# Seven-product MLP2 extended from the last two groups to groups 2 to 5, with accumulator banks seeded by ScalarE copies

## The chip, the cores and the metric

One core of one Trainium2 chip. The metric is the device time of one execution in microseconds (us). With one core there is no second die to compare, so a run is called slow here only when it lies over 1.5% above the fastest of its kernel. The kernel before takes 373.25 us (median of the 3 runs before the prediction, 373.15 to 373.69). Times in the profile count from the first instruction of the span, which is about 2 us shorter than the run.

Names: PE is the TensorE matmul engine, DVE is VectorE, ACT is ScalarE, POOL is GpSimd, SP is SyncE, which issues most DMAs. PSUM is the memory in which PE accumulates; it is handed out in tiles, here of two banks each. The granted clock is the share of full speed at which PE's clock ran. Groups are counted from 0 to 7 as in the code; the words of the change count them from 1, so its "groups 3 to 6" are 2 to 5 here.

## The reference

```python
x = A_x                                          # 1 x 2048 x 576, bf16
h = x + A(layernorm(x), wqkv, wo)                # dilated local attention: 32 heads, window 8, step 2
y = layernorm(layernorm(h))                      # the MLP normalises its input once more
h2 = h + gelu(y @ w1 + b1) @ w2 + b2             # w1: 576 x 4608, w2: 4608 x 576
```

The 2048 rows are 16 tiles of 128. A group is two of these tiles. For each of the 8 groups PE does MLP1 (324 matmuls, in four visits; ACT applies the Gelu), then Wo, the attention's output projection, for the next group (36), then MLP2. LN2 is the doubled layernorm: its rows go through the DMA that transposes them (`hnT`) into the next MLP1. Attention for the group after that runs on DVE at the same time.

## The kernel before: the parts that matter

MLP2 of a group multiplies hidden blocks by the w2 blocks of one "block row", 18 times over:

    | A11 A12 |   | B11 B12 |      A: 2 tiles x 2 hidden blocks,  B: 2 hidden blocks x 2 halves of the columns
    | A21 A22 | x | B21 B22 |

Plainly that is 8 matmuls a block row, 144 a group. The Strassen-Winograd scheme needs 7 products, so 126 a group. It pays with sums of hidden blocks and weight blocks on DVE, and with partial results that two output quarters share. The kernel before has this scheme in groups 6 and 7 only. Where a quarter is to continue from a partial sum, ACT copies the PSUM bank into another bank, in which PE goes on accumulating ("seeding").

```python
    # mlp2_fast of the kernel before, groups 6 and 7 (cut)
        call(ahead[:1])                                   # Wo of the next group
        af, b = (psum_pair(tag, "po") for tag in tags[:2])
        if not last:
            product(1, af[:, 0, 0:HALF], True)
            nc.scalar.copy(out=b[:, 0, 0:HALF], in_=af[:, 0, 0:HALF])     # seed b from bank a
        call(ahead[1:])                                   # LN2 of the next group
        ...
        ce, d = (psum_pair(tag, "po") for tag in tags[2:])    # b and d are two tiles
        bank = {1: a, 2: a, 3: f, 4: c, 5: d, 6: b, 7: e}
        then = {1: [c_(nc.scalar.copy, b, a)], 6: [c_(nc.scalar.copy, d, b)], ...}
        if last:
            order = [(1, 0, cut), (4, 0, cut), (1, cut, NM), (4, cut, NM)] + [(n, 0, NM) for n in (7, 6, 2, 5, 3)]
        else:
            order = [(n, 0, NM) for n in (4, 2, 6, 7, 5, 3)]   # product 4, in bank c, stands between 1 and 2
```

```python
    # the loop over the groups, groups 2 to 5 (cut)
                    ...
                    m1[1] = [c_(att_qk_pair, e, f)]
                    ia[0] = [c_(exps, e, f), wo, c_(ln2_pair, c, d, (e, f)), ...]
            mlp1(g, "pair", m1, mid)
            mlp2_tile(g, 0, "D", ia)          # 72 plain matmuls each
            mlp2_tile(g, 1, "C", ib)
    def exps(*js):
        att_exp(*js)          # ACT: Exp, with its table load
        gelu_table()          # ACT: a tiny Gelu, which loads the Gelu table again
```

## Time and profile before

| | before |
|---|---|
| time, median | 373.25 us |
| span of the profiled run, granted clock | 370.7 us, 1.00 |
| PE busy; matmuls | 98%; 4944 |
| a plain group: MLP1, Wo, MLP2 | 17.79, 2.21, 17.75 us |
| MLP2 of group 6 (126 matmuls) | 15.54 us |
| DVE busy in the MLP2 of groups 2 to 5 | 14.7 to 16.4 of 17.7 to 18.2 us |

The page of the kernel before, its busy times and two rows of its 40 slices (a digit is tenths of a slice; PEclk is the granted clock):

```profile
PE 363.6 (98%) x4944; PEld 299.1 (81%) x4944; DVE 286.9 (77%) x415; ACT 225.5 (61%) x499; POOL 41.1 (11%) x47
PE   8999999999999999999999999999999999999996
PEclk9999999999999999999999999999999999999999
```

All that PE waited for, in the list of waits (total, times, longest):

```profile
PE busy L695 <- DVE prod L688: 1.5, 1, 1.5
PE pm L214 <- ACT hT L524: 0.5, 1, 0.5
PE o_pt L181 <- DVE h L432: 0.5, 1, 0.5
PE pm L214 <- DMA hnT<-td: 0.5, 1, 0.5
PE pq L214 <- ACT kv_ring L299: 0.2, 1, 0.2
```

PE is the limit: 3.2 us of waits in 370.7. A matmul taken out there is time won, as long as PE isn't made to wait. What ACT does around the end of MLP1: its timeline in group 3, where PE's MLP1 ends and Wo starts at 202.44 (start, duration, what):

```profile
200.74 4.49 ACT L524 ACTIVATE hT<-pm,b_sb 128x256 bf16<-128x256 f32 x12 [1.99 <-PE pm L214]
205.25 1.28 ACT L366 ACT_TABLE_LOAD   x1
206.54 0.63 ACT L366 ACTIVATE logits<-logits 128x512 f32<-128x512 f32 x1
207.19 1.28 ACT L497 ACT_TABLE_LOAD   x1
208.49 0.20 ACT L497 ACTIVATE warm<-mhalf 128x1 f32<-128x1 f32 x1
```

ACT ends its Gelus 2.8 us after PE ends MLP1, and is then taken by the exponentials until 6.25 us after it. In this kernel nobody waits for that: PE goes on with Wo and the plain MLP2. And where the kernel before does seed a bank (group 6), PE doesn't wait either. The copy, in ACT's timeline, and PE's matmuls under it:

```profile
320.80 0.39 ACT L621 COPY po<-po 128x288 f32<-128x288 f32 x1 [1.82 <-PE po L610]
```

```profile
320.05 0.65 PE L610 MATMUL po<-w2b_sb,hT 128*128 128x288 bf16 x4
320.54 1.14 PE L610 MATMUL po<-kv_ring,hT 128*128 128x288 f16 x8
```

The matmuls from 320.54 on are product 4, which has a bank of its own.

### The profile page before, as it was taken

How to read it: one execution, taken by the hardware profiler on the slowest of the kernel's cores; microseconds unless marked ns; L12 is line 12 of the kernel's file. 1: busy time of each engine (PE TensorE's matmuls, PEld its weight loads, DVE VectorE, ACT ScalarE, POOL GpSimd, SP SyncE). 2: the span in 40 equal slices, each digit the busy share in tenths (PEclk: the TensorE clock that was granted, in tenths of full speed). 3: DMA queues.
4: the chain of work that ended last, by engine and by line, in shares of the span. 5: the costliest groups of instructions: out<-in, count | busy, mean ns of one | idle time of the engine just before them, and what ended most of it. 6: DMA issues, size and time to landing. Idle time of an engine off the chain costs nothing.

```text
span 370.7 us, 11474 instructions
## 1 busy us (share of the span) xinstructions
PE 363.6 (98%) x4944; PEld 299.1 (81%) x4944; DVE 286.9 (77%) x415; ACT 225.5 (61%) x499; POOL 41.1 (11%) x47
## 2 busy tenths in 40 slices
PE   8999999999999999999999999999999999999996
PEld 4689877888788877887788778877887888778884
DVE  6799999999999959999686989598959883532332
ACT  2688755798738790679166915692468436735630
POOL 2322004000220011003100011001100210000000
PEclk9999999999999999999999999999999999999999
DMA  7969798956557725600471145313820361030001
GB/s 230 316 180 307 190 200 229 336 181 75 173 168 137 257 87 85 102 18 34 104 120 51 34 104 105 66 33 99 106 53 18 85 121 37 0 88 19 4 0 32
DMA packets 60722, 42.51 MB, mean 115 GB/s; under 512 B 31728, under 2 KB 58992, under 8 KB 60672
## 3 DMA queue, kind: packets, MB, share of 16 engines
q1 hardware_dynamic: 58784, 39.95, 40.8%
q0 software_dynamic: 1728, 1.77, 4.8%
q8 instruction: 38, 0.62, 0.7%
q10 hardware_dynamic: 160, 0.07, 0.1%
q14 instruction: 12, 0.10, 0.1%
HBM read 19.92 MB, written 12.42 MB: 87 GB/s over the span
## 4 chain that ended last, share of the span: by engine, by line
PE 80%; DVE 14%; ACT 2%; DMA 1%; issue 1%; SPq 1%; POOL 0%; DVEq 0%; POOLq 0%
PE pm L214 35%; PE po L539 24%; PE po L610 8%; PE pq L214 6%; PE pw L214 4%; DVE prod L332 2%; DVE prod L381 2%; DVE prod L326 2%; DVE prod L385 2%; PE busy L695 1%; ACT hT L524 1%; DVE x_all L573 1%; DMA hnT<-td 1%; PE xt_pt L181 1%; DVE peak L344 1%
## 5 line engine op out<-in xcount | busy, mean ns | idle before, releaser
L524 ACT ACTIVATE hT<-pm,b_sb 128x256 bf16<-128x256 f32 (+1 forms) x288 | 108.6, 497 | 86.8 <-PE pm L214 86.8
L214 PE MATMUL pm<-hnT,w_sb 64*128 64x256 bf16 x2304 | 143.0, 269 | 0.9 <-ACT hT L524 0.5
L214 PEld LDWEIGHTS <-w_sb 64*128 64x128 bf16 x2304 | 112.4, 94 | 15.6 <-issue 2.1
L539 PEld LDWEIGHTS <-hT 128*128 128x128 bf16 x864 | 84.0, 98 | 22.6 <-issue 1.7
L539 PE MATMUL po<-w2a_sb,hT 128*128 128x288 bf16 x672 | 84.5, 286 | 0.0
L214 PE MATMUL pq<-wq_sb,xnT 64*128 64x288 bf16 x768 | 54.3, 283 | 0.3 <-ACT kv_ring L299 0.2
L214 PEld LDWEIGHTS <-xnT 64*128 64x128 bf16 x864 | 43.9, 94 | 9.3 <-ACT xnT L260 0.4
L326 DVE TENSOR_TENSOR prod<-kv_ring,q_all 128x4608 bf16<-128x4608 bf16 x16 | 40.8, 2549 | 13.2 <-DMA kv_ring<-kv_dram 13.1
L381 DVE TENSOR_TENSOR prod<-kv_ring,probs 128x4608 bf16<-128x4608 bf16 x16 | 40.9, 2558 | 7.8 <-DMA kv_ring<-kv_dram 7.4
L332 DVE TENSOR_TENSOR prod<-prod 128x2304 bf16<-128x2304 bf16 (+1 forms) x64 | 44.2, 691 | 2.1
L214 PE MATMUL pm<-hnT,w1h_sb 64*128 64x256 bf16 x288 | 39.3, 269 | 0.0
L448 POOL TENSOR_TENSOR ln_rstd<-ln_var,mhalf 128x1 f32<-128x1 f32 x14 | 16.1, 1151 | 190.3 <-ACT ln_var L447 190.3
L385 DVE TENSOR_TENSOR prod<-prod 128x2304 bf16<-128x2304 bf16 (+1 forms) x32 | 33.9, 1058 | 1.1
L539 PE MATMUL po<-w2b_sb,hT 128*128 128x288 bf16 x192 | 25.5, 286 | 0.0
L299 ACT CAST kv_ring<-pq 128x576 bf16<-128x576 f32 x32 | 19.5, 642 | 8.2 <-PE pq L214 8.2
L586 DVE TENSOR_TENSOR prod<-hT 128x512 f16<-128x512 f16 (+1 forms) x8 | 3.7, 458 | 21.6 <-ACT hT L524 21.6
L214 PE MATMUL pw<-wo_sb,oT 64*128 64x288 bf16 x256 | 19.5, 283 | 0.2
L161 POOL TENSOR_TENSOR ln_rstd<-ln_veps,mhalf 128x1 f32<-128x1 f32 (+2 forms) x13 | 13.3, 1026 | 49.3 <-DVE ln_veps L155 40.3
L214 PEld LDWEIGHTS <-oT 64*128 64x128 bf16 x288 | 13.9, 94 | 4.3 <-POOLq L224 0.8
L469 POOL DMA_DIRECT2D x_all<-h x12 | 10.9, 1060 | 44.4 <-DMA td<-q_all 30.2
L214 PEld LDWEIGHTS <-w1h_sb 64*128 64x128 bf16 x288 | 14.1, 94 | 1.6
L150 DVE BATCH_NORM_STATS2 ln_stats<-x_all 128x6 f32<-128x288 bf16 x32 | 12.8, 443 | 2.4 <-DMA x_all<-in_A_x_dram 2.4
(99 smaller groups left out, 326.3 us busy)
## 6 DMA issues: line engine op xcount, KB each, us to landing
w_sb<-in_B_w_dram SPq DMA_DIRECT2D x6, 768.0 KB, 6.1
kv_ring<-kv_dram SPq DMA_DIRECT2D x28, 144.0 KB, 2.6
w2a_sb<-in_B_w_dram SPq DMA_DIRECT2D x4, 1008.0 KB, 6.5
kv_dram<-kv_ring SPq DMA_DIRECT2D x13, 288.0 KB, 4.6
out_dram<-o_sb SPq DMA_DIRECT2D x15, 144.0 KB, 3.1
td<-q_all SPq DMA_DIRECT2D x14, 144.0 KB, 2.0
td<-hn SPq DMA_DIRECT2D x14, 144.0 KB, 1.8
wq_sb<-in_A_wqkv_dram SPq DMA_DIRECT2D x3, 576.0 KB, 6.6
```

The source lines that it names most:

```text
L150: nc.vector.bn_stats(out=stats[:, i, c, :], in_=src[:, c * HALF:(c + 1) * HALF])
L161: nc.gpsimd.tensor_tensor(out=rstd[:], in0=veps[:], in1=mhalf[:].to_broadcast([P, n]), op=ALU.pow)
L214: last = nc.tensor.matmul(duo["g"][r ^ swap][i], lhsT=lhsT, rhs=rhs, start=(swap == 0 and i == 0 and kt == 0), stop=(swap == 1 and kt == K ...
L299: pace[0] = nc.scalar.copy(out=dst.rearrange("p (d g h) -> p g d h", g=2, h=H // 2), in_=ps[:, :, 0:HALF].rearrange("p g (h d) -> p g d h" ...
L326: nc.vector.tensor_tensor(out=prod[:], in0=k_ring[j % 2], in1=q_all[:, j, :].unsqueeze(1) .to_broadcast([P, W, D]), op=ALU.mult)
L332: nc.vector.tensor_tensor(out=prod[:, :, o * H:o * H + n], in0=prod[:, :, a * H:a * H + n], in1=prod[:, :, c * H:c * H + n], op=ALU.add)
L381: nc.vector.tensor_tensor(out=prod[:].rearrange("p w (d h) -> p w d h", h=H), in0=v_ring[j % 2].rearrange("p w (d h) -> p w d h", h=H), in ...
L385: nc.vector.tensor_tensor(out=prod[:, 0:n, :], in0=prod[:, 0:n, :], in1=prod[:, n:2 * n, :], op=ALU.add)
L448: nc.gpsimd.tensor_tensor(out=rstd[:], in0=var[:], in1=mhalf[:], op=ALU.pow)
L524: pace[0] = nc.scalar.activation(out=hT[us[i // GF]][:, GF * r + i % GF, 0:N], in_=ps[:, r, i * N:(i + 1) * N], func=ACT.Gelu_apprx_tanh, ...
L539: nc.tensor.matmul(banks[half], lhsT=hT[f // (2 * GF)][:, f % (2 * GF), i * P:(i + 1) * P], rhs=w2_rows(f)[:, half * HALF:(half + 1) * HAL ...
L610: nc.tensor.matmul(bank, lhsT=l, rhs=r, start=(start and m == 0), stop=(m == NM - 1), skip_group_check=True)
```

## The change

The intent: seven products for the first 8, 8, 12 and 12 of the 18 block rows of groups 2 to 5 too, 40 matmuls fewer. The rest of the diff finds room for it: weight sums partly in place of a w2 quarter or in odd slots of x (so x of the odd tiles is loaded again later, into even slots), hidden sums partly in place, one sum taken in each group. All seven-product groups now use five banks in three PSUM tiles, with three seeds each, instead of six banks in four tiles.

```diff
+    def x_of(j):
+        return x_all[:, j - j % 2, :]
+    def reload_x(js):
+        for j in js:
+            nc.sync.dma_start(out=x_of(j), in_=x3[:, j, :])
...
-    fast = GROUPS[-2:]
+    fast = GROUPS[2:]
...
+        af, bd, ee = (psum_pair(tag, "po") for tag in tags)
+        a, f, b, d = (pair[:, n, 0:HALF] for pair in (af, bd) for n in range(2))
+        e = ee[:, 0, 0:HALF]
...
+        product(1, a, rows, True)
+        seed(b, a)                      # nc.scalar.copy
+        call(inserts.get(1, ()))        # LN2 statistics, hidden sums
+        product(2, a, rows)             # the same bank a
+        plain(0, 0, a, rows)            # the block rows that stay plain
...
+        product(6, b, rows)
+        seed(d, b)
+        call(inserts.get(6, ()))        # LN2 rows normalised (ACT) and sent
+        product(7, e, rows, True)
...
+        product(5, d, rows)
+        seed(f, d)
+        product(4, b, rows)
+        plain(1, 0, b, rows)
+        plain(1, 1, d, rows)
...
+        product(3, f, rows)
+        plain(0, 1, f, rows)
...
+        ROWS = {2: 8, 3: 8, 4: 12, 5: 12, 6: NM, 7: NM}
...
+            mlp1(g, mlp1_plan(p, q, r, s, True), m1, mid)
+            if e is not None:
+                exps(e, f)
+            if c is not None:
+                wo_visit((c, q), (d, r))
+            mlp2_fast(g, rows, (s, p, q), c is None, x)
```

## The prediction

> **What bounds it now.** TensorE: the busy summary gives PE 98% of a 370.7 us span, granted clock 9 or more in all slices, and the list of waits finds only 3.2 us of PE waiting. A plain group of two block rows is 37.7 us by the chain (MLP1 17.79, Wo 2.21, MLP2 17.75: 144 matmuls, so 123 ns each). The two seven-product groups need 126 matmuls, 15.54. VectorE is busy 31 to 33 of 37.7 us in each of the groups 2 to 5 (counted from 0; table of windows), ScalarE 23.
>
> **Removed.** With r of 18 rows by seven products a group has 144 - r matmuls: r = 8, 8, 12, 12 saves 40, at 123 ns 4.9 us (estimate from the above). All of it lies on the critical path. The 0.5 us PE wait for the transposed LN2 rows before group 6 should also go.
>
> **Added, off the path.** Sums of hidden blocks on VectorE: 0.42 us for 512 elements and 0.55 for 768, so about 0.69 and 0.95 at 1024 and 1536; four per group, 2.8 to 3.8 us. The weight sums only move; those in group 1 (6 x 0.75) fill its 4.2 us wait for the exponentials. VectorE ends near 300 us in all. Reloads of x: four groups, 2 x 144 KB each, at a DMA share of about 0.35. Seed copies: 18 of 0.385 us.
>
> **Added, on the path.** The first seed is the flaw. Product 1 is followed directly by product 2 into the same bank, but ScalarE has to copy that bank in between, so PE waits for it. The present kernel runs product 4 meanwhile. And in groups 2 to 5 ScalarE comes late: its timeline in group 3 shows the last Gelu ending 2.8 us after MLP1's last matmul (202.44 to 205.25), then two table loads around the exponentials (1.28 + 0.63 + 1.28 + 0.20) until 208.7. The Trainium skill's page "ScalarE: Activation LUTs", section "What ACT_TABLE_LOAD costs", gives about 1283 ns for one; this trace agrees (1283 ns). The copy stands behind all that: free at +6.3, done at +6.65, PE on at about +6.75. PE reaches it at 2.2 (Wo) + 1.0 (8 matmuls) = +3.2, or +3.7 with 12. Stall 3.55, 3.55, 3.05, 3.05: 13.2 us. Group 6 has no exponentials: product 1 ends at +4.4, copy and handshake about 0.65. Group 7: no Wo either, product 1 complete only near the last Gelu, +1.1.
>
> Sum: 373.25 - 4.9 - 0.5 + 13.2 + 1.75 = 382.8.
>
> **Prediction:** 382.8 us, 8 in 10 between 378 and 387. Faster by over 2%: 0.03; within 2%: 0.20; slower by over 2%: 0.77.
>
> **What would show it.** In the list of waits, PE waits for the ScalarE seed copy, six times: four of 3 to 3.6 us, two near 1. The chain passes in groups 2 to 5 from PE through the last Gelus, both table loads, the exponentials and the copy back to PE. PE has 40 fewer matmuls at an unchanged 123 ns spacing. VectorE idles longer than before in these groups. The next group's MLP1 doesn't wait for VectorE's output sums.
>
> **What would make it wrong.** ScalarE being less late than I reckon would bring it near 376. VectorE's order (output sum behind the weighted sums of V, 5.2 us) is within about 1 us of holding the second MLP1 visit; if it does, add 1 to 2 us a group. The skill's "TensorE: Matmul & The Clock Gate", Part 1, has the clock drop after an idle window of about 3.4 us; the stalls are that long, and the clock row would show it. If the copy doesn't hold product 2 at all, about 369.

## The result, and the profile after

The change is slower: 392.85 us median (389.87 to 396.85, 4 runs, one of them slow) against 373.2 for the kernel before (4 runs). The ratio is 1.0504 (95% interval 1.0424 to 1.0584). A ratio is the mean time of one kernel's fast runs over that of the other's of the same rounds, so not quite the ratio of the medians. The direction was predicted; the size was not: 19.6 us lost for 9.6 predicted. The granted clock of the four runs, 0.995, 0.977, 0.990 and 0.977, goes roughly with their times, 389.87, 394.31, 391.39 and 396.85.

The profiled run is the fastest of them. Its busy times and slices:

```profile
PE 361.8 (93%) x4904; PEld 297.3 (77%) x4904; DVE 298.3 (77%) x412; ACT 229.8 (59%) x513; POOL 35.1 (9%) x47
PE   7999999999999998968998799979997999999895
PEclk9999999999999999989999999999999999999999
```

There are 40 matmuls fewer, and PE is busy 93% instead of 98%. PE's waits:

```profile
PE po L619 <- ACT po L650: 17.2, 12, 3.3
PE busy L721 <- DVE prod L714: 1.5, 1, 1.5
PE po L619 <- ACT h_all L528: 1.4, 1, 1.4
PE pm L214 <- DVE o_sb L692: 1.0, 1, 1.0
...
```

Line 650 is the seed copy. PE waits for it twelve times, not six. PE's own timeline shows where, in groups 2 and 3 (the idle time before a piece stands in brackets):

```profile
167.44 1.16 PE L619 MATMUL po<-w2a_sb,h_all 128*128 128x288 bf16 x8
171.89 4.28 PE L619 MATMUL po<-w2a_sb,h_all 128*128 128x288 bf16 x20 [3.29 <-ACT po L650]
...
181.10 0.65 PE L619 MATMUL po<-x_all,h_all 128*128 128x288 f16 x4 [1.00 <-ACT po L650]
...
214.95 2.61 PE L619 MATMUL po<-w2a_sb,h_all 128*128 128x288 bf16 x20 [3.30 <-ACT po L650]
```

The piece at 167.44 is product 1, that at 171.89 product 2. So the first wait is there as predicted. The piece at 181.10 is product 4, whose wait the prediction does not have. And the same 20 matmuls take 4.28 us in group 2 and 2.61 in group 3: in group 2 the clock has fallen. The table of windows shows it (window, its length, then busy us and instructions of PE, PEld, DVE, ACT and POOL, granted clock, DMA share, GB/s):

```profile
168.97:172.39 3.42, 0.50 (x5) 0.39 (x5) 3.38 (x6) 3.38 (x7) 0.00 (x0) 1.00 0.24 86
172.39:175.80 3.41, 3.41 (x17) 2.18 (x15) 2.59 (x4) 3.15 (x10) 0.56 (x1) 0.50 0.00 0
```

PE was idle for 2.92 us of the first window, and in the second it ran at half the clock. ACT's timeline for the first wait has the chain that the prediction named, in the place of the five lines shown of before (PE's MLP1 ended at 165.2):

```profile
163.60 4.49 ACT L528 ACTIVATE h_all<-pm,b_sb 128x256 f16<-128x256 f32 x12 [1.99 <-PE pm L214]
168.11 1.28 ACT L366 ACT_TABLE_LOAD   x1
169.40 0.63 ACT L366 ACTIVATE logits<-logits 128x512 f32<-128x512 f32 x1
170.05 1.28 ACT L504 ACT_TABLE_LOAD   x1
171.34 0.20 ACT L504 ACTIVATE warm<-mhalf 128x1 f32<-128x1 f32 x1
171.45 0.39 ACT L650 COPY po<-po 128x288 f32<-128x288 f32 x1
```

And for the wait of product 4, the third copy behind the two LN2 rows:

```profile
178.17 0.38 ACT L650 COPY po<-po 128x288 f32<-128x288 f32 x1 [2.50 <-PE po L619]
178.47 0.30 ACT L460 ACTIVATE ln_nmean<-ln_nmean,ln_rstd 128x1 f32<-128x1 f32 x1
178.80 0.87 ACT L174 ACTIVATE hn<-h,ln_nmean,ln_rstd 128x576 bf16<-128x576 f32 x1
179.57 0.28 ACT L460 ACTIVATE ln_nmean<-ln_nmean,ln_rstd 128x1 f32<-128x1 f32 x1
179.88 0.87 ACT L174 ACTIVATE hn<-h,ln_nmean,ln_rstd 128x576 bf16<-128x576 f32 x1
180.66 0.39 ACT L650 COPY po<-po 128x288 f32<-128x288 f32 x1
```

Product 4 writes bank b; that copy only reads bank d and writes bank f. In the built program, product 5 waits until ACT's counter has reached 221 (the second copy, which fills d), and product 4 until it has reached 226: the four LN2 instructions and the third copy. Banks b and d are the two halves of one PSUM tile, `bd`.

The stages that changed, each from its first matmul to the first of the next stage (us, worked out from the matmuls' start times in the traces; the experiments' columns are used below):

| stage | before | after | control | fill | fill + split | product 1 twice |
|---|---|---|---|---|---|---|
| MLP2, group 2 | 17.75 | 23.06 | 22.73 | 21.56 | 20.39 | 18.62 |
| MLP2, group 3 | 17.75 | 21.39 | 23.05 | 21.56 | 20.39 | 18.62 |
| MLP2, group 4 | 17.75 | 19.88 | 19.87 | 20.04 | 19.41 | 17.75 |
| MLP2, group 5 | 18.27 | 19.88 | 21.54 | 20.04 | 19.41 | 17.75 |
| MLP2, group 6 | 15.54 | 16.86 | 16.86 | 16.86 | 16.22 | 16.22 |
| group 7 to the end | 36.84 | 39.59 | 39.57 | 39.58 | 38.95 | 38.96 |

The 18.27 of before holds its wait of 0.5 us for the LN2 rows of group 6.

The ideal for groups 2 and 3 is 136 matmuls at 0.123 us, 16.8 us, and 16.3 for 4 and 5 (estimates from the spacing before).

### The profile page after: what moved, and what is told of

It reads as the page before. It is cut to its first block, busy times and chain, and to the rows that moved or that the text cites. A ratio compares the mean times of both kernels' runs of the same rounds, so it can differ in the third digit from the quotient of the medians.

```text
span 388.1 us, 11433 instructions
## 1 busy us (share of the span) xinstructions
PE 361.8 (93%) x4904; PEld 297.3 (77%) x4904; DVE 298.3 (77%) x412; ACT 229.8 (59%) x513; POOL 35.1 (9%) x47
## 4 chain that ended last, share of the span: by engine, by line
PE 51%; DVE 32%; ACT 7%; issue 4%; DMA 2%; SPq 1%; POOL 1%; DVEq 0%; ACTq 0%; POOLq 0%
PE pm L214 25%; PE po L619 24%; DVE prod L381 5%; DVE prod L332 5%; DVE prod L326 5%; DVE prod L385 4%; ACT h_all L528 3%; DVE ln_stats L150 2%; PE pw L214 2%; DVE h L439 1%; DMA x_all<-in_A_x_dram 1%; ACT po L650 1%; ACT L504 1%; DVE peak L344 1%; PE pq L214 1%
## 5 line engine op out<-in xcount | busy, mean ns | idle before, releaser
L528 ACT ACTIVATE h_all<-pm,b_sb 128x256 f16<-128x256 f32 (+1 forms) x288 | 108.5, 498 | 94.4 <-PE pm L214 94.4
L619 PEld LDWEIGHTS <-h_all 128*128 128x128 f16 x560 | 55.1, 99 | 36.3 <-issue 22.2
L619 PE MATMUL po<-w2a_sb,h_all 128*128 128x288 bf16 (+1 forms) x332 | 47.3, 293 | 14.7 <-ACT po L650 13.3
L542 PEld LDWEIGHTS <-h_all 128*128 128x128 bf16 x288 | 28.0, 98 | 7.7 <-issue 0.7
L542 PE MATMUL po<-w2a_sb,h_all 128*128 128x288 bf16 x224 | 28.3, 286 | 0.0
L455 POOL TENSOR_TENSOR ln_rstd<-ln_var,mhalf 128x1 f32<-128x1 f32 x14 | 10.3, 733 | 198.2 <-ACT ln_var L454 196.8
L619 PEld LDWEIGHTS <-kv_ring 128*128 128x128 f16 x228 | 22.3, 98 | 5.6
L599 DVE TENSOR_TENSOR kv_ring<-h_all 128x1536 f16<-128x1536 f16 (+2 forms) x8 | 6.3, 786 | 21.4 <-ACT h_all L528 21.4
L619 PE MATMUL po<-w2b_sb,h_all 128*128 128x288 bf16 (+1 forms) x152 | 22.2, 286 | 0.0
L650 ACT COPY po<-po 128x288 f32<-128x288 f32 x18 | 6.9, 386 | 19.8 <-PE po L619 19.8
```

The source lines that it names most:

```text
L455: nc.gpsimd.tensor_tensor(out=rstd[:], in0=var[:], in1=mhalf[:], op=ALU.pow)
L528: pace[0] = nc.scalar.activation(out=hT(grp)[:, f, 0:N], in_=ps[:, r, i * N:(i + 1) * N], func=ACT.Gelu_apprx_tanh, bias=b1_sb[:, f:f + 1] ...
L542: nc.tensor.matmul(banks[half], lhsT=hT(grp)[:, f, i * P:(i + 1) * P], rhs=w2_rows(f)[:, half * HALF:(half + 1) * HALF], start=(f == 0), s ...
L619: nc.tensor.matmul(bank, lhsT=l, rhs=r, start=start, stop=stop, skip_group_check=True)
L650: nc.scalar.copy(out=to, in_=bank)
```

## The experiments

The theory after the traces: the loss has three parts, (A) the wait for the first copy, as predicted; (B) a wait of product 4 that comes of two banks sharing one tile; (C) a TensorE clock that falls because of the waits. Rivals: the scatter and the extra loss come from the work that the change added elsewhere (DVE sums, x reloads, DMA queue), or product 4 really needs that copy. All ten kernels gave correct results. The first four ran together; so did fill and split together, product 1 twice and Wo between (on another chip), and late exponentials filled with the second of the versions that keep the saving (on a third). Across these jobs, compare the ratios to the kernel before.

### Control: the changed kernel once more

> The changed kernel once more, unaltered, as the control for the three runs beside it. Expected as measured: 388 to 397 us, scattered, mean granted clock 0.97 to 1.0 and lower in the slower executions; PE waits for the ScalarE copies about 18 us in all.

No edit. Measured 393.48 us (392.59 to 394.54, clock 0.981 to 0.990), ratio to before 1.0577 (1.0552 to 1.0602). In its profile, groups 2, 3 and 5 lost clock; group 4 did not (19.87 in the table, as in the run after). So the loss is stable, and a low clock comes with it.

### Fill: useless matmuls in place of the idle time

> Changed kernel plus 24 (groups 2, 3) or 20 (groups 4, 5) useless matmuls put before product 1, in its own bank, so that PE works through the time in which it would otherwise wait for the first seed copy. The copy still comes at 6.25 us after MLP1, behind the Gelus and the exponentials, so the chain is as long as before. Theory A (the stalls of about 3.3 us also let the TensorE clock drop, and that is the scatter and about 5 to 6 us of the loss): time falls to about 386.5 us, scatter under 1 us, clock 1.00, although PE has 88 matmuls (10.8 us) more to do. Rival B (the scatter has another source, and the whole loss is waits): no faster than the control, about 390 to 393, or slower.

```diff
+        for _ in range({8: 24, 12: 20}.get(rows, 0)):
+            mm(a, h_block(0, 0, 0, 1), w2_block(0, 0, 0, 1), True, True)
         product(1, a, rows, True)
         seed(b, a)
```

Measured 388.46 us (388.29 to 391.05), clock 0.999 to 1.000 in all runs: 5.0 us faster than the control with 88 matmuls more. PE's timeline in group 2:

```profile
166.91 4.09 PE L619 MATMUL po<-w2a_sb,h_all 128*128 128x288 bf16 x32
171.53 2.61 PE L619 MATMUL po<-w2a_sb,h_all 128*128 128x288 bf16 x20 [0.53 <-ACT po L650]
```

Product 2 starts at nearly the same moment as before (4.62 us after the first matmul of the stage, 4.45 in the changed kernel), since the copy still comes when ACT gets to it. But its 20 matmuls take 2.61 us. So theory C holds: the idle time costs once as a wait and a second time as a slow clock. It came out 2 us above the expected 386.5; the expectation doesn't say how that was summed, so why stays open. One of the four runs (391.05) lies 2.5 us above the others at a clock of 0.999; that is not explained either.

### Split: banks b and d in two tiles

> Changed kernel with the two banks b and d of the second block row in two PSUM tiles instead of one; nothing else but that its output sum becomes two. In the built program product 4, which writes bank b, waits for the third seed copy, which only reads bank d. Theory (this wait is one of tile bookkeeping, not of data): the wait of product 4 (1.0, 1.0, 0.47 four times, 3.9 us in the profile) vanishes and the time falls by 3.5 to 4 us against the control of the same rounds, so far as the scatter lets it be seen; the first-seed waits stay at 2.8 to 3.3 us. Rival (product 4 needs that copy, or another wait takes its place): no change.

```diff
-        af, bd, ee = (psum_pair(tag, "po") for tag in tags)
-        a, f, b, d = (pair[:, n, 0:HALF] for pair in (af, bd) for n in range(2))
-        e = ee[:, 0, 0:HALF]
+        af, bb, ee, dd = (psum_pair(tag, "po") for tag in tags)
+        a, f = (af[:, n, 0:HALF] for n in range(2))
+        b, e, d = (pair[:, 0, 0:HALF] for pair in (bb, ee, dd))
...
-        add(halves(o1[:]), bd[:, :, 0:HALF], rest)
+        for n, bank in enumerate((b, d)):
+            add(o1[:, n * HALF:(n + 1) * HALF], bank, rest[:, n, :])
```

Measured 390.4 us (388.58 to 390.68), 3.1 less than the control, and with a clock that is still low (0.978 to 0.982). PE's list of waits:

```profile
PE po L619 <- ACT po L650: 13.2, 6, 3.3
```

Six waits instead of twelve; those of product 4 are gone and nothing has taken their place. The results were right without that wait, so it was bookkeeping: theory B holds. The Trainium skill's page "PSUM — Partial Sum Buffer", section "Terms", forbids two engines only on the same bank at once, and b and d are two banks; the run agrees: in group 2 PE wrote b from 180.47 to 181.61 us while ACT's third copy, from 181.20 on, read d. The time fell by 3.1 and not 3.9, because more of the clock was lost here (0.978 to 0.982 for 0.981 to 0.990; its trace has falls in all of groups 2 to 5, the control's in three).

### The exponentials behind the first copy

> Changed kernel with the exponentials issued on ScalarE behind the first seed copy instead of in front of it, in groups 2 to 5. The first wait should fall from 3.3 and 2.8 us to about 0.5 in each of these groups, which shows that it is the ScalarE queue and not the copy that makes it long. But ScalarE then has 3.4 us more to do before the second seed copy: estimate from the measured durations, product 5 waits 2.2 us (groups 2, 3) or 1.8 us (4, 5) and product 4 1.7 or 1.0, so the waits move instead of going: 4.4 us a group for 4.3, and 3.3 for 3.3. Time about 386 us with a clock of 1.00[...]. If the waits do go and are not replaced, about 374 to 378.

```diff
             if e is not None:
-                exps(e, f)
+                x[1] = [c_(exps, e, f)] + x[1]
```

Measured 396.93 us (396.33 to 397.79): slower, not 386. The waits moved as estimated. PE's timeline in group 2:

```profile
168.79 2.61 PE L619 MATMUL po<-w2a_sb,h_all 128*128 128x288 bf16 x20 [0.53 <-ACT po L650]
...
176.34 0.65 PE L619 MATMUL po<-x_all,kv_ring 128*128 128x288 f16 x4 [1.99 <-ACT po L650]
...
179.59 1.06 PE L619 MATMUL po<-x_all,h_all 128*128 128x288 f16 x4 [2.11 <-ACT po L650]
180.44 1.17 PE L619 MATMUL po<-q_all,h_all 128*128 128x288 f16 x4
```

The first wait falls to 0.53 us: it is the queue on ACT that makes it long, not the copy. The same work on ACT then holds products 5 and 4 (1.99 and 2.11 us in group 2, for 2.2 and 1.7 estimated). Two things in the expectation were wrong. In groups 4 and 5 product 4 waited 2.11 and 1.93 us, for 1.0 estimated, so that all waits for the copies came to 19.3 us, 2.2 more than in the control. And the clock was not 1.00: it fell (0.978 to 0.983) although no wait was longer than 2.1 us, and the last two lines show 4 matmuls at 1.06 and 1.17 us, for 0.65. So a fall does not need a single gap of about 3 us.

### Late exponentials, with the waits filled

> The kernel with the exponentials behind the first copy (396.9 us, clock 0.978 to 0.983, although no wait in it was longer than 2.1 us) with useless matmuls in a spare bank before product 5 (14, or 11 in groups 4 and 5) and before product 4 (14), each set a little shorter than the wait that it stands in. Theory (the clock falls when PE has been busy too small a part of a few microseconds, so two waits of 2 us with 1 us of work between them do it as well as one of 3.3): clock 1.00, and the time falls by 5 to 7 us to 390 to 392, with the same waits in sum as filled work. Rival (the clock falls for another reason, or only after a single long gap): clock stays at 0.98 and the time at 396 to 398.

```diff
+        useless(14 if rows == 8 else 11)      # matmuls into a spare bank
         product(5, d, rows)
         seed(f, d)
         call(inserts.get(5, ()))
+        useless(14)
         product(4, b, rows)
```

Measured 391.47 us (390.4 to 391.56), clock 0.999 to 1.000, with 106 matmuls more. The ratio to before is 1.0496 (1.0458 to 1.0533), for 1.0676 (1.0658 to 1.0694) without the filling: the theory's numbers came true. The two waits together, which it blamed, are not what the trace shows. Narrow windows of the kernel without the filling, in group 2:

```profile
172.86:176.27 3.41, 1.48 (x13) 1.05 (x11) 3.25 (x5) 3.28 (x11) 0.69 (x2) 1.00 0.00 0
176.27:179.69 3.42, 1.25 (x9) 0.87 (x9) 3.35 (x3) 2.56 (x6) 1.74 (x1) 1.00 0.17 48
179.69:183.10 3.41, 3.41 (x16) 2.15 (x15) 0.56 (x2) 0.00 (x0) 0.00 (x0) 0.50 0.56 139
```

The first window has the wait of product 5 and PE idle for 1.93 us: no fall. The second has that of product 4 and PE idle for 2.17: half the clock follows. In group 3 the wait of product 5 (1.99 us) was enough alone. Every fall in groups 2 to 5 lasts 3.41 us, or twice that, and the falls of one trace start whole multiples of 3.41 us apart. So the clock seems to be set window by window, and the windows don't begin with a wait. (Idle time of a window is its length less PE's busy time.) In the window before each of the 11 falls (4 traces) PE was idle for 1.99 to 3.08 us; of all other windows at full clock in the twelve traces, up to the last products, the idlest has 2.03 us and the next 1.93. So about 2 us of idle time in one window of 3.41 us let the clock fall, in one wait or several (worked out from modelled ends of matmuls, after the runs; no run moved the windows on purpose). The same reading fits a wait of 3.3 us that cost clock in group 2 of the changed kernel and not in group 3: there the windows cut the idle time into 1.70 and 1.61 us. Which waits are hit would then be luck of the run, which would explain why the times scatter; that is not shown.

### Fill and split together

> Both of the earlier alterations at once: the useless matmuls before product 1, which kept the clock at 1.00 (388.5 us against 393.5 for the control), and banks b and d in two tiles, which took the wait of product 4 away (waits for the copies 13.2 instead of 17.1 us). If these are the two things that the prediction left out, and they are independent, the time is that of the prediction, 382.8, plus what group 7 costs above its estimate (about 1): 383 to 384.5 us, clock 1.00, no wait at product 4. If one hides the other, 385 to 388.

The two edits above in one kernel. Measured 383.86 us (383.56 to 384.14), clock 0.998 to 1.000. With parts B and C taken away, the time is that of the prediction and one microsecond. The two parts don't hide one another: 393.48 (control) to 388.46 by the fill, to 383.86 by the split on top. The steps depend on the order, though, since the split alone brought 3.1 us and then left 6.5 to the fill: the more clock is lost, the less a removed wait shows. (The last kernel is from another chip job, in which the kernel before took 373.38 instead of 372.14, so the step of 4.6 could be up to 1.2 more.)

### Product 1 computed twice instead of copied

> Banks b and d in two tiles, and in groups 2 to 5 product 1 is computed a second time into bank b, so that no first copy is needed there. That costs as many matmuls as the seven products save (each of these groups has 144 again). Theory (the loss is the PE wait for the first copy, with the clock drop that it brings): groups 2 to 5 fall to about 17.75 us of MLP2 (4, 5) or up to 18.6 (2, 3, where the second copy stands behind the LN2 sums on ScalarE), so 375 to 377 us in all, the rest being the waits in groups 6 and 7; clock 1.00. Rival (the loss lies in the other work that the change added on VectorE, ScalarE and the DMA queue): the waits reappear under another name and the time stays above 382.

```diff
         product(1, a, rows, True)
-        seed(b, a)
+        if rows < NM:
+            product(1, b, rows, True)
+        else:
+            seed(b, a)
```

(on top of the split). Measured 377.31 us (376.81 to 377.44), 0.3 above the expected range; ratio 1.0105 (1.0081 to 1.0129). The stages are as expected: 18.62, 18.62, 17.75, 17.75. With as many matmuls as the plain group has, and no first copy, groups 4 and 5 take what a plain group takes. So the added sums, reloads and copies cost nothing themselves there, and the rival that blames them is out for these stages. What is left of the loss is the 0.7 us waits for the second copy in groups 2 and 3, and groups 6 and 7.

### A version that keeps the saving

> A version that keeps the saving. In groups 2 to 5 product 1 comes first, in the bank that ScalarE frees first; the Wo matmuls (2.2 us) run between it and product 2, under the first copy; the exponentials stand behind that copy, one LN2 row behind the second copy; banks b and d in two tiles. Groups 6 and 7 keep the order of products of the kernel before. Estimate from the measured durations: no wait at product 2, at most 0.5 us at product 5, 0 at product 4; the next group's LN2 rows arrive up to 0.6 us late. So MLP2 and Wo about 19 to 19.6 us a group against 20.0 before: 368 to 371 us, clock 1.00, 0.5 to 1 per cent faster than before. If the ScalarE queue as a whole is too long for this order, waits at products 5 and 6 or for the LN2 rows bring it to 372 to 376.

```diff
+        product(1, a, rows, True)                  # right after MLP1, in the bank that ACT frees first
+        nc.scalar.copy(out=b, in_=a)
+        call(x.get(1, ()))                         # exponentials (ACT), two hidden sums (DVE)
+        wo()                                       # 36 matmuls under the copy
...
+        product(2, a, rows)
...
+        product(6, b, rows)
+        nc.scalar.copy(out=d, in_=b)               # between the statistics of the two LN2 rows
```

(b and d in two tiles; groups 6 and 7 in the order of the kernel before.) Measured 373.1 us (372.32 to 375.27), ratio 1.0009 (0.9965 to 1.0054): the same as before. No wait at product 2, and group 4 took 16.56 us of MLP2 (1.58 for product 1, 14.98 for the rest), close to the ideal. But PE waited 1.69 us in group 2 and 0.68 in group 3 for the third copy, 1.0 us for DVE's output sum in the MLP1 of group 2, and 0.8 us for the LN2 rows of group 6. The expected 368 to 371 was missed.

### The same with two of these waits taken out

> The version with Wo between products 1 and 2, with two waits that its profile showed taken out: the third seed copy now stands between the two normalised LN2 rows on ScalarE instead of behind both (PE waited 1.69 us for it in group 2 and 0.68 in group 3), and one of the six weight sums of group 1 moves into group 2, where VectorE held up the second MLP1 visit by 0.97 us. Expected: 373.1 less 1.7, 0.7 and 0.7, so 370.0 us (369.3 to 371.0), and 0.4 to 0.8 per cent faster than the kernel before in the same rounds; the wait for LN2 rows before group 6 (0.8 us) stays. If the LN2 rows get later through the copy, waits for them appear before groups 3 and 4 too and it stays at 371.5 to 373.

```diff
-            x[6] = [..., c_(ln2_send, c), c_(ln2_send, d)]
+            x[6] = [..., c_(ln2_send, c)]
+            x[5] = [c_(ln2_send, d), ...]               # so the third copy stands between the two rows; x[7]'s inserts moved here too
-            [c_(w2_sums, m, m + 4, (0, 1, 3)) for m in (0, 4)]
+            [c_(w2_sums, 0, 4, (0, 1, 3)), c_(w2_sums, 4, 8, (0, 1))]     # the sixth sum follows in group 2
```

Measured 372.51 us (371.19 to 373.65), ratio 0.9984 (0.9955 to 1.0013): still the same. The expectation's other branch came true. The waits for the copies are gone from the list, and others stand there:

```profile
PE pm L214 <- DMA hnT<-td: 1.9, 3, 1.1
PE busy L767 <- DVE prod L760: 1.5, 1, 1.5
PE pm L214 <- DVE prod L381: 1.4, 1, 1.4
```

`hnT` are the LN2 rows for the next MLP1. The waits before groups 4, 5 and 6 are 0.25, 0.55 and 1.11 us. A shorter MLP2 reaches the next MLP1 before its input is there: the saving had become a new wait. (The line with `prod` is at the same place, the start of group 3's MLP1.)

### The LN2 rows hurried

> The last version with the LN2 rows hurried, because its profile shows that the matmuls of the next MLP1 now wait for them (1.4, 0.3, 0.6 and 1.1 us at groups 3 to 6): the reload of the V ring, which stands in front of the two transposing reads in the SyncE queue (0.55 us of it, and more where it waits for VectorE), is issued from the ScalarE queue, and in groups 4 and 5 the third copy stands behind both LN2 rows again. Theory (the SyncE queue and the ScalarE order are the last part of the LN2 chain): the four waits fall by about 0.5 us each where they are there, 371.0 us, 0.3 to 0.6 per cent faster than before. Rival (the chain is held by the exponentials and table loads earlier on ScalarE and by GpSimd, which this leaves alone): 372 to 373, no different from the kernel before.

```diff
+            x[6 if rows > 8 else 5] += [c_(ln2_send, d)]
-            x[5] = [c_(ln2_send, d), c_(att_pv_sum, e), c_(halo, e, 2), c_(ln2_ins, c, d), ...]
+            x[5] += [c_(att_pv_sum, e), c_(halo, e, 2, nc.scalar), c_(ln2_ins, c, d), ...]   # issued by ACT
```

Measured 370.36 us (369.82 to 371.62), ratio 0.9936 (0.9917 to 0.9956): 0.6% faster than the kernel before, which is clear of the noise here. Its busy times and what is left of PE's waits:

```profile
PE 359.7 (98%) x4904; PEld 300.2 (82%) x4904; DVE 300.2 (82%) x423; ACT 228.7 (62%) x511; POOL 35.8 (10%) x47
```

```profile
PE busy L767 <- DVE prod L760: 1.5, 1, 1.5
PE pm L214 <- DVE o_sb L738: 0.9, 1, 0.9
PE pm L214 <- ACT h_all L528: 0.5, 1, 0.5
...
PE pm L214 <- DVE prod L381: 0.3, 1, 0.3
...
```

The theory held: the waits for the LN2 rows fell from 3.3 us (1.9 and 1.4) to 0.3. Wo and MLP2 of groups 2 to 5 take 19.67, 19.34, 18.70 and 18.77 us, for 20.05 three times and 20.57 in the kernel before: 4.2 us less in sum. About 1.1 us is given back in group 2's MLP1 (18.83 for 17.70), whose second visit waits for DVE. Two edits were made at once here, so how much each of them brought stays open.

## Why the prediction was wrong

**Right.**

- The plan saves 40 matmuls (4944 to 4904), and PE was the limit before.
- The wait for the first copy, with its size: 3.55, 3.55, 3.05 and 3.05 us predicted, 3.29, 3.30, 2.81 and 2.81 idle measured. The profile counts idle time from the modelled end of a matmul, which lies 0.16 us behind its turn (0.286 long at 0.123 spacing), so the two agree within 0.1 us.
- Its cause. The copy stands behind the Gelus, two table loads and the exponentials. The Trainium skill's page "ScalarE: Activation LUTs", section "What ACT_TABLE_LOAD costs", gives about 1283 ns for a load, and the traces show 1283 ns. Putting the exponentials behind the copy left 0.53 us of the wait.
- DVE near 300 us (298.3), and the wait of 0.5 us for LN2 rows gone.

**Wrong: the sum "373.25 - 4.9 - 0.5 + 13.2 + 1.75 = 382.8" lacked two terms, and one was too small.**

1. "PE on at about +6.75" took the first copy to be the only one that PE waits for ("six times" in "What would show it"). There are twelve waits. Product 4 waits for the third copy because banks b and d share a tile, and the order on ACT (both LN2 rows before that copy) makes it up to 1.0 us. Without it: 4.6 us less (388.46 to 383.86, with the reserve made there); the waits of product 4 alone sum to 3.9 us in the control's profile.
2. "PE has 40 fewer matmuls at an unchanged 123 ns spacing" took the clock to stay at 1.00; its fall was named under what would make it wrong and not put into the sum. It did fall, in one of groups 2 to 5 in the first profile of the changed kernel and in three in the control's. Each fall costs about 1.7 us (20 matmuls in 4.28 us instead of 2.61). In all 5.0 us: 393.48 for the control, 388.46 with the waits filled.
3. "Group 7: ... +1.1" was 2.1 (38.95 for 36.84, with the tiles split): PE waits 1.4 us for the last Gelu and then 0.5 for the copy, so the two add.

The parts close. Predicted 382.8; with parts 1 and 2 taken away, measured 383.86, of which part 3 explains 1.0. That 4.6 and 5.0 us on top make the control's 393.48 is so by construction. The traces give a check of their own: 3.9 us of waits of product 4 and three falls, each 3.41 us at half the clock, so 5.1 us, on top of the profiled 383.87 make 392.9, and the control's profiled run took 392.83 (an estimate; smaller waits of the two differ by some tenths). "The next group's MLP1 doesn't wait for VectorE's output sums" was nearly right: it waited once, in group 2, for 1.0 us in this profile and 0.5 in the control's. The weight sums moved in front of them may delay them; that is not shown, since taking one of these sums away left 0.4 us in one version and 0.9 in the next.

**Where the expected gain went.** Removing the first copy by computing product 1 twice spends just the matmuls that the seven products save (377.31, with the tiles split). The saving of 4.9 us came out only after the copy was hidden under Wo, the tiles split, the copies moved in ACT's order and the LN2 rows hurried. Then 370.36 us, 2.5 us less than the kernel before in the same rounds. The first two of the three versions show why it takes all of that: each wait taken away was replaced by the next one.

## What to carry to other kernels

Before an accumulator bank is copied and then accumulated into again, ask what stands in front of that copy in the copying engine's queue at that moment, and put independent matmuls between the two. Where PE is the limit, idle time of 2 us or more within 3.41 us is to be counted twice, as the wait and as the clock that may fall after it: here about 1.7 us for each fall, and by luck not after every such wait. Give banks that different engines use at different times tiles of their own, since the waits may follow the tile and not the bank.

## What the Trainium skill lacked or had wrong

- "TensorE: Matmul & The Clock Gate", Part 1, has the clock fall after an idle window of about 3.4 us, and its section "Why this matters for your kernels" warns of gaps over about 3 us. Here the windows before a fall were not wholly idle: 1.99 to 3.08 of 3.41 us were enough, and single waits of 1.99 and 2.11 us did it. The page doesn't give the share of a window that PE must be idle. What one fall costs agrees with the page's half rate for about 3.4 us: 1.67 us lost in the piece of 20 matmuls.
- The same page doesn't say that a wait can be filled with useless matmuls to hold the clock: 88 of them made the kernel 5.0 us faster, at a clock of 1.00.
- "ScalarE: Activation LUTs", section "What ACT_TABLE_LOAD costs", adds about 1380 ns of drain to every load, 2.66 us in all. In these traces the load starts right behind the last Gelu (205.23 to 205.25) and the Exp 0.01 us behind the load, so a switch costs 1.31 us.
- No page has that two banks in one PSUM tile are waited for together by the tile framework: 12 waits for the copies, 17.1 us in all, with one tile, and 6, 13.2 us, with two.
